# Deferred block products: operand steps issued a block ahead, and the second output weight combined in the last chunk and the first group

## The chip, the cores and the metric

The kernel runs on one core of one Trainium2 chip. TensorE (PE) multiplies out of SBUF into PSUM, ScalarE (ACT) and VectorE (DVE) split operands and move results, GpSimd (POOL) does a few SBUF-only operations, and every transfer (DMA) is issued by SyncE (SP), so all of them stand in one queue of issue. Each engine works through its own list of instructions in order and waits on semaphores for the others. The metric is device microseconds (us) for one execution; a change of about 0.2% (3.4 us) can be told from no change.

## The reference

```python
# attention through 32 packed tokens per head, B=8, H=8, S=576, D=64
p_packed = sm_attn(p, k, v)                 # softmax(p k^T / 8) v
x = sm_attn(q, p_packed, p_packed)          # -> 4608 tokens x 512
# first feed-forward: 512 -> 1536 -> 512
xn = x / rms(x) * rms_g
x = (silu(xn @ w_gate) * (xn @ w_val)) @ w_out
# second feed-forward: 512 -> 2048 -> 512, per-column leaky slope alpha
h = x @ w_in
out = (max(h, 0) + alpha * min(h, 0)) @ w_out
```

All inputs are float32. Every matrix product is done in three passes: an operand is split into a rounded high part and the rest, and high*high, high*low and low*high are added up (`mm3`).

## The kernel before

**First phase.** The 4608 tokens are walked in 12 chunks: chunks 0, 4, 7 and 10 have 512 tokens, the others 320. A chunk loops over 12 slices f of the hidden width. In a slice PE makes gate and value (`blk_in`), ACT applies a tanh or a silu (L1047 and L1049), DVE multiplies (L1052, L1056), the product is split by `hsplit` (high part on ACT L109, rest on DVE L112), and one slice later PE multiplies it with the output weight (`blk_out`). Between these the attention of the next chunk is worked in by hand-written turns (`work`, `burst`, `wg_job`). Chunk results go to `y_dram`. The last chunk has no attention beside it; there `prep(0)` makes the operands of the second phase's first group.

**The late weights.** `late` is a generator (`conv_late`) that turns the second feed-forward's weights, 8 pairs of row blocks of each, into operands. `work` calls it once in every slice of chunks 1 to 10. For a pair it takes seven steps: three that load and unpack two blocks (`narrow`), and four in `sevenths` that form the seven combinations a seven-product (Strassen-type) scheme needs. For a combination, `product` has ACT write the high part into a tile `w7o`, POOL subtract to get the rest (L275), and SP store the tile (256 KB) to DRAM: `w7_dram` for w_in, `o7_dram` for w_out. POOL also forms the sums and differences between (`combine`, L279). There are two `w7o` tiles (`bufs=2`), so the split of a combination waits until the store of the one two before it has landed. The last of the four steps makes three combinations at once: 6, 5 and 3 for w_out (6, 5 and 2 for w_in).

**Second phase.** Five groups of token pairs (`PAIRS`: three of 2 x 512, two of 2 x 384). Within a group a loop over i = 0 to 7 makes seven input products (`prod`, 6 matmuls each, in the order 0, 5, 4, 6, 1, 2, 3) into three PSUM banks a, b_ and c_. ACT copies product 0 out of a into `m1` (L1202); product 1 is then accumulated onto the same bank a, so on PE it follows that copy. ACT and DVE make the leaky activation (`halves_of`, `prelu`), and two output blocks of an earlier i run in between (`fill`). After the loop the other 40 output blocks follow, the list `LATER`: eight each of the kinds 5, 2, 6, 3, 1. A block (`block`) splits its operand (ACT, then DVE) and appends its 12 matmuls (9 in the narrow groups) to `fill`; they are issued once more than `LAG = 3` blocks wait. For kind 2 the operand is first formed in place by DVE:

```python
if n == 2:
    less2(s2, h21, s2)          # DVE L1132
block(x, n, i, g, w, ...)       # ACT split, DVE rest
```

Weight tiles are loaded in the order of their use by `load_next`, twelve ahead; each load is issued behind the PE work that frees its buffer. The ring of 2 x 2 buffers for split operands lets a block's split begin when the block four before it has left PE. The rows call both `w7_dram` and a scratch copy by names without digits: `w_dram<-w7o` is a store of w_in's combinations, `o_dram<-w7o` one of w_out's.

Of the kernel before, what the change touches and what calls it, by code (L numbers as in the profile page):

```python
# [18 lines left out]
def attention_moe_moe2_kernel(ctx, tc, q, k, v, p, w_gate, w_val, w_out, rms_g, w_in2, w_out2, alpha, out):  # L19
# [72 lines left out]
    gv_dram = tc.dram_tile([NJ * 4, 128, 512], F32, name="gv_dram")  # L92
    lo_dram = tc.dram_tile([NF, 128, 512], F32, name="lo_dram")
    w7_dram = tc.dram_tile([NP2 * 7, 128, 2, 256], F32, name="w7_dram")
    o7_dram = tc.dram_tile([NP2 * 7, 128, 2, 256], F32, name="o7_dram")
# [12 lines left out]
    def split_hi(hi, src):  # L108
        nc.scalar.activation(out=hi, in_=src, func=ACTF.Copy)  # L109
# [15 lines left out]
    with tc.manual_schedule():  # L125
# [124 lines left out]
        def conv_late():  # L250
            ahead = [load_wide(u, one, NST) for u in units2[:2]]
            yield
            for m in range(0, len(units2), 2):
                pair = []
                for n in (m, m + 1):
                    pair.append(one.tile([128, 4, 128], F32, tag="w32", name="w32", bufs=2))
                    steps = narrow(ahead.pop(0), pair[-1])
                    next(steps)
                    yield
                    for _ in steps:  # L260
                        pass
                    if n + 2 < len(units2):
                        ahead.append(load_wide(units2[n + 2], one, NST))
                yield
                yield from sevenths(*units2[m], pair)

        def sevenths(kind, i, pair):
            blocks = [t.rearrange("p c x -> p (c x)")[:, h * 256:(h + 1) * 256] for t in pair for h in range(2)]
            b11, b12, b21, b22 = blocks
# [615 lines left out]
        LATER = [(x, n, i) for x, n in (("b", 5), ("c", 2), ("b", 6), ("d", 3), ("a", 1)) for i in range(NP2)]  # L885
        LAG = 3

# [37 lines left out]
        for c, (t0, n, cuts) in enumerate(CH):  # L925
# [9 lines left out]
            def work(f, at):  # L935
# [18 lines left out]
                if c == 0:  # L954
                    conv(2 if at < 4 else 0)
                elif not last and at == 3:
                    next(late, None)

# [66 lines left out]
            for f in range(NF):  # L1025
# [9 lines left out]
                if last:  # L1035
                    if f == 0:
                        y_rows.append(load_rows(0, 0))
                        prepare = prep(0)
                    if f > 0:
                        next(prepare, None)  # L1040
                    if f in (2, 3, 8, 9, 10):
                        next(prepare, None)
                    load_next()
                tg = blk_in(f, 0, "g")
# [101 lines left out]

        def split2(g, w):
            n_h[0] += 1
            hh, hl = [
                ring.tile(  # L1150
                    [128, T], F32R, tag="ho"[n_h[0] % 2] + x, name="h" + x, bufs=NRO[x] if n_h[0] % 2 else 2
                )[:, 0:w]
                for x in "hl"
            ]
            split_hi(hh, g)
            split_lo(hl, g, hh)
            return hh, hl

        acc = {}

        def banks(x, j):
# [4 lines left out]
        def block(x, n, i, g, w, first, last, then=None):  # L1166
            hh, hl = split2(g, w)

            def run_block():
# [8 lines left out]
                if then:  # L1178
                    then()
            fill.append(run_block)  # L1180

        def pieces(w):
            return [(j, min(T, w * 2 - j * T)) for j in range((w * 2 + T - 1) // T)]

        for pr, (t0, w) in enumerate(PAIRS):
            final = pr + 1 == len(PAIRS)
            late_h, waiting = {}, []
            for i in range(NP2):
# [3 lines left out]
                def prod(o, n, first):  # L1192
# [4 lines left out]
                    load_next()  # L1197

                a, b_, c_ = [bank("g")[:, 0:w] for _ in range(3)]
                prod(a, 0, True)  # L1200
# [5 lines left out]
                for f_ in waiting:  # L1206
                    f_()
                prod(c_, 4, True)
                prod(b_, 6, False)
                u3 = temp(w)  # L1210
# [7 lines left out]
                n22 = halves_of(h22, h22, w)  # L1218
                prelu(h22, n22, i + NP2)
                fill.pop(0)()  # L1220
                prod(c_, 2, False)
                h12 = temp(w)
                add2(h12, u2, c_)
                block("a", 0, i, g11, w, i == 0, i == NP2 - 1)
                n12 = halves_of(h12, h12, w)
                prod(b_, 3, False)
                h21 = keep(1, i, w)
                add2(h21, m1, b_)
# [6 lines left out]
                n21 = halves_of(h21, h21, w)  # L1235
                late_h[i] = (h22, h21, s2, s3)
                fill.pop(0)()
                waiting = [
                    lambda h=h21, n=n21, f=i + NP2: prelu(h, n, f),
                    lambda s=s1, i=i, w=w: block("c", 4, i, s, w, i == 0, i == NP2 - 1),  # L1240
                ]
# [49 lines left out]
            prepare = iter(()) if final else prep(pr + 1)  # L1291
            for k_, (x, n, i) in enumerate(LATER):
                h22, h21, s2, s3 = late_h[i]
                if n == 2:
                    less2(s2, h21, s2)
                g = {5: s2, 2: s2, 6: s3, 3: h22, 1: h21}[n]
                then = None
                if i == NP2 - 1:
                    then = {5: done_b6, 2: done_c, 6: done_b7, 3: done_d, 1: lambda d=done_a, e=final: d(e)}[n]
                block(x, n, i, g, w, n in (5, 3) and i == 0, i == NP2 - 1, then)  # L1300
                while len(fill) > LAG:
# [44 lines left out]
```

## Time and profile before

| what | us |
|---|---|
| median of 3 runs (1713.65 to 1713.99) | 1713.79 |
| the profiled execution's own time | 1711.09 |
| its span, from the first to the last instruction | 1709.2 |
| chunks 1, 2, 3, 5, 6, 8, 9 (320 tokens) together | 489.3 |
| chunks 4, 7, 10 (512 tokens) together | 250.3 |
| chunk 11, the last | 42.8 |
| first group of the second phase | 166.5 |
| PE busy | 1601.2 |

The profile's busy time of PE counts overlapping matmuls with modelled ends, so PE can be late without showing as idle; the spacing of equal work tells more. ACT is busy 893.1 us and DVE 1147.2 us of the span.

### The profile page before, as it was taken

What the parts mean: (1) busy time and instruction counts of PE and PEld (TensorE: products, weight loads), DVE (VectorE), ACT (ScalarE), POOL (GpSimd) and SP (SyncE); (2) the same over time, 40 slices, a digit from 0 to 9 for tenths busy, and PEclk for the clock granted to TensorE, in tenths of its full rate; (3) what the DMA queues carried; (4) which work ended last, traced back from release to release, by engine and by line L of the source; (5) the groups of instructions that cost most, each with busy time, mean ns of one, the idle gap of its engine ahead of it and who ended that gap; (6) DMA issues with size and microseconds to landing.
All of it is one profiled execution on the core that took longest, in us unless ns stands there. A gap on an engine that the chain in (4) does not pass through costs nothing.

```text
span 1709.2 us, 31979 instructions
## 1 busy us (share of the span) xinstructions
PE 1601.2 (94%) x11786; PEld 1395.5 (82%) x11786; DVE 1147.2 (67%) x2132; ACT 893.1 (52%) x1906; POOL 339.6 (20%) x350
## 2 busy tenths in 40 slices
PE   6789999888999899999999999999999999999998
PEld 4457877777877787778888888888898889998998
DVE  5786656655566656556646677867777777777775
ACT  4566555554455454555545555544554544554553
POOL 1441344453445532233200000000000000000000
PEclk8899999999999999999999999999999999999999
DMA  9876656635456565675525666677566757877875
GB/s 255 257 251 193 186 168 204 179 114 180 158 179 206 158 202 181 213 237 172 178 88 190 179 196 197 216 204 215 166 222 203 210 154 236 259 247 252 260 227 179
DMA packets 230426, 340.55 MB, mean 199 GB/s; under 512 B 62464, under 2 KB 96256, under 8 KB 230272
## 3 DMA queue, kind: packets, MB, share of 16 engines
q1 hardware_dynamic: 230272, 338.51, 64.5%
q8 instruction: 94, 1.54, 0.4%
q14 instruction: 60, 0.49, 0.1%
HBM read 280.77 MB, written 57.67 MB: 198 GB/s over the span
## 4 chain that ended last, share of the span: by engine, by line
PE 62%; DVE 15%; ACT 8%; issue 6%; DMA 5%; POOL 3%; SPq 1%; ACTq 0%; DVEq 0%; POOLq 0%
PE ps_g L121 11%; PE ps_g L122 11%; PE ps_g L123 11%; PE ps_y L121 6%; PE ps_y L123 6%; PE ps_y L122 6%; DVE hl L112 2%; ACT hh L109 2%; PE ps_wg L731 2%; DMA w_dram<-w7o 2%; PE ps_v L121 2%; PE ps_v L122 1%; PE ps_v L123 1%; DVE kept L1132 1%; DVE s L1056 1%
## 5 line engine op out<-in xcount | busy, mean ns | idle before, releaser
L121 PE MATMUL ps_y<-hh,in_h 128*128 128x320 f32 (+1 forms) x576 | 207.9, 361 | 3.5 <-ACT hh L109 3.5
L121 PE MATMUL ps_g<-yh,w 128*128 128x512 f32 (+1 forms) x560 | 206.5, 369 | 0.0
L122 PE MATMUL ps_g<-yl,w 128*128 128x512 f32 (+1 forms) x560 | 206.3, 368 | 0.0
L123 PE MATMUL ps_g<-yh,w 128*128 128x512 f32 (+1 forms) x560 | 205.7, 367 | 0.0
L122 PE MATMUL ps_y<-hl,in_h 128*128 128x320 f32 (+1 forms) x576 | 196.9, 342 | 5.0 <-DVE hl L112 4.5
L123 PE MATMUL ps_y<-hh,in_l 128*128 128x320 f32 (+1 forms) x576 | 195.9, 340 | 0.6 <-DMA in_l<-lo_dram 0.6
L1052 DVE SCALAR_TENSOR_TENSOR s<-s,ps_g 128x320 f32<-128x320 f32 (+1 forms) x132 | 71.3, 540 | 166.1 <-ACT s L1047 165.8
L109 ACT ACTIVATE hh<-kept 128x512 fp32r<-128x512 f32 (+1 forms) x200 | 115.0, 586 | 129.1 <-DVE kept L1132 56.3
L121 PE MATMUL ps_y<-w,hh 128*128 128x256 f32 x576 | 167.5, 291 | 12.6 <-ACT hh L109 12.5
L123 PE MATMUL ps_y<-w,hl 128*128 128x256 f32 x576 | 168.3, 292 | 9.9 <-DVE hl L112 9.1
L122 PE MATMUL ps_y<-w,hh 128*128 128x256 f32 x576 | 164.8, 286 | 0.0
L112 DVE TENSOR_TENSOR hl<-kept,hh 128x512 fp32r<-128x512 f32 (+1 forms) x200 | 122.3, 635 | 60.1 <-ACT hh L109 59.7
L109 ACT ACTIVATE hh<-s 128x320 fp32r<-128x320 f32 (+1 forms) x144 | 75.6, 525 | 162.1 <-DVE s L1056 162.0
L121 PEld LDWEIGHTS ps_y<-hh,in_h 128*128 128x128 f32 x576 | 109.6, 190 | 58.7 <-issue 43.2
L275 POOL TENSOR_TENSOR w7o<-w,w7o 128x256 fp32r<-128x256 f32 x112 | 88.9, 800 | 205.9 <-ACT w7o L109 202.9
L121 PEld LDWEIGHTS ps_y<-w,hh 128*128 128x128 f32 x576 | 111.7, 194 | 19.1 <-ACT hh L109 16.6
L1129 DVE TENSOR_TENSOR tmp<-tmp,ps_g 128x512 f32<-128x512 f32 (+2 forms) x140 | 87.5, 631 | 58.3 <-PE ps_g L123 56.8
L112 DVE TENSOR_TENSOR hl<-s,hh 128x320 fp32r<-128x320 f32 (+1 forms) x144 | 85.8, 596 | 60.7 <-ACT hh L109 60.7
L123 PEld LDWEIGHTS ps_y<-w,hl 128*128 128x128 f32 x576 | 112.1, 195 | 15.8 <-DVE hl L112 15.7
L123 PE MATMUL ps_g<-w,hl 128*128 128x256 f32 x432 | 124.1, 287 | 0.4 <-DVE hl L112 0.4
L121 PE MATMUL ps_g<-w,hh 128*128 128x256 f32 x432 | 124.3, 288 | 0.0
L122 PE MATMUL ps_g<-w,hh 128*128 128x256 f32 x432 | 124.2, 287 | 0.0
(193 smaller groups left out, 4279.9 us busy)
## 6 DMA issues: line engine op xcount, KB each, us to landing
w<-w_dram SPq DMA_DIRECT2D x280, 256.0 KB, 3.0
w<-o_dram SPq DMA_DIRECT2D x280, 256.0 KB, 2.9
gv_raw<-gv_dram SPq DMA_DIRECT2D x168, 256.0 KB, 3.9
in_l<-lo_dram SPq DMA_DIRECT2D x59, 256.0 KB, 3.1
w<-in_moe_w_out_dram SPq DMA_DIRECT2D x28, 512.0 KB, 5.5
w_dram<-w7o SPq DMA_DIRECT2D x56, 256.0 KB, 2.1
o_dram<-w7o SPq DMA_DIRECT2D x56, 256.0 KB, 2.1
vt<-in_v_dram SPq DMA_DIRECT2D x16, 576.0 KB, 5.4
```

The costliest lines, as they stand in the source:

```text
L109: nc.scalar.activation(out=hi, in_=src, func=ACTF.Copy)
L112: nc.vector.tensor_tensor(out=lo, in0=src, in1=hi.bitcast(F32), op=ALU.subtract)
L121: nc.tensor.matmul(out=o, lhsT=lh, rhs=rh, start=first, stop=False, skip_group_check=more)
L122: nc.tensor.matmul(out=o, lhsT=lh, rhs=rl, start=False, stop=False, skip_group_check=more)
L123: nc.tensor.matmul(out=o, lhsT=ll, rhs=rh, start=False, stop=last, skip_group_check=more)
L275: nc.gpsimd.tensor_tensor(out=t[:, 1], in0=src, in1=t[:, 0].bitcast(F32), op=ALU.subtract)
L731: nc.tensor.matmul(out=ts[g][h * NP:(h + 1) * NP, :], lhsT=ppG[b][e * D:(e + 1) * D, c_, :], rhs=us[c_][e * D:(e + 1) * D, :], start=True, ...
L1052: nc.vector.scalar_tensor_tensor(out=s, in0=s, scalar=1.0, in1=tg, op0=ALU.add, op1=ALU.mult)
L1056: nc.vector.tensor_tensor(out=s, in0=s, in1=tv, op=ALU.mult)
L1129: nc.vector.tensor_tensor(out=out, in0=x, in1=y, op=ALU.add)
L1132: nc.vector.tensor_tensor(out=out, in0=x, in1=y, op=ALU.subtract)
```

## The change

It has three parts. First, in `LATER` a block is now a generator with two steps: the ACT split, and the DVE rest with the append to `fill`. The steps of neighbouring blocks are interleaved: DVE's `less2` for block k+2, ACT's split for k+1, DVE's rest for k. `LAG` goes from 3 to 2. Second, `conv_late` only unpacks w_out's pairs and stores them unsplit to a new scratch `w_dram` (two stores of 256 KB a pair); a new generator `make_o7` loads a pair back (512 KB into a `w64` tile) and then does the four steps of `sevenths`. It is called once at the start of each of the 12 slices of the last chunk and five times in every i of the first group (`make`), 40 steps in all. Third, `late` is called in every second slice of the 320-token chunks; in the 512-token chunks in every slice, and twice in every fourth.

```diff
+                kind, i = units2[m]
+                if kind == "o2":
+                    for e in range(2):
+                        nc.sync.dma_start(out=w_dram[i, :, e], in_=pair[e].rearrange("p c x -> p (c x)"))
                 yield
-                yield from sevenths(*units2[m], pair)
+                if kind == "i2":
+                    yield from sevenths(kind, i, [t.rearrange("p c x -> p (c x)") for t in pair])
+
+        def make_o7():
+            for i in range(NP2):
+                t = one.tile([128, 2, 512], F32, tag="w64", name="o2_raw", bufs=NST)
+                nc.sync.dma_start(out=t, in_=w_dram[i])
+                yield
+                yield from sevenths("o2", i, [t[:, e] for e in range(2)])
...
-        LAG = 3
+        LAG = 2
...
-                elif not last and at == 3:
-                    next(late, None)
+                elif not last and at == 3 and (f % 2 or n == T):
+                    for _ in range(1 + (n == T and f % 4 == 3)):
+                        next(late, None)
...
                     if f in (2, 3, 8, 9, 10):
                         next(prepare, None)
+                    next(making)
                     load_next()
...
+        def make(pr):
+            if pr == 0:
+                next(making, None)
...
-            hh, hl = split2(g, w)
+            hh, hl = split_tiles(w)
+            split_hi(hh, g)
+            yield
+            split_lo(hl, g, hh)
...
             fill.append(run_block)
+            yield
...
+                make(pr)
                 a, b_, c_ = [bank("g")[:, 0:w] for _ in range(3)]
                 prod(a, 0, True)
...
                 prod(c_, 4, True)
+                make(pr)
                 prod(b_, 6, False)
...
                 prelu(h22, n22, i + NP2)
+                make(pr)
                 fill.pop(0)()
...
                 prod(b_, 3, False)
+                make(pr)
                 h21 = keep(1, i, w)
...
                 late_h[i] = (h22, h21, s2, s3)
+                make(pr)
                 fill.pop(0)()
...
+            def combine_next(k_):
+                if k_ < len(LATER) and LATER[k_][1] == 2:
+                    _, h21, s2, _ = late_h[LATER[k_][2]]
+                    less2(s2, h21, s2)
+
+            next(splits[0])
+            for k_ in range(len(LATER)):
+                combine_next(k_ + 2)
+                if k_ + 1 < len(LATER):
+                    next(splits[k_ + 1])
+                next(splits[k_])
                 while len(fill) > LAG:
```

**Where instructions stand, 1: DVE in the kind-2 blocks of the first group.** `kept<-kept,kept` is `less2` for a kind-2 block, `hl<-kept,hh` the rest of a split, `tmp<-tmp,ps_g` the reading of kind 5's sums out of PSUM, `y_d` and `yl` belong to `prep` of the next group. Before:

```order
L1132 TENSOR_TENSOR kept_11612<-kept_11607,kept_11612 128x512
L112 TENSOR_TENSOR hl_12720<-kept_11612,hh_12719 128x512
L1132 TENSOR_TENSOR kept_11750<-kept_11745,kept_11750 128x512
L112 TENSOR_TENSOR hl_12739<-kept_11750,hh_12738 128x512
L1132 TENSOR_TENSOR kept_11882<-kept_11877,kept_11882 128x512
L112 TENSOR_TENSOR hl_12758<-kept_11882,hh_12757 128x512
L1129 TENSOR_TENSOR tmp_12775<-tmp_12582,ps_g_12618 128x512
L1129 TENSOR_TENSOR tmp_12777<-tmp_12584,ps_g_12625 128x512
L856 TENSOR_TENSOR y_d_12779<-y_raw_12295,y_raw_12293 128x512
L112 TENSOR_TENSOR yl_12782<-y_d_12712,yh_12781 128x512
```

With the change:

```order
L1148 TENSOR_TENSOR kept_11815<-kept_11810,kept_11815 128x512
L113 TENSOR_TENSOR hl_12747<-kept_11477,hh_12746 128x512
L1148 TENSOR_TENSOR kept_11979<-kept_11974,kept_11979 128x512
L113 TENSOR_TENSOR hl_12772<-kept_11649,hh_12771 128x512
L1145 TENSOR_TENSOR tmp_12808<-tmp_12614,ps_g_12644 128x512
L1145 TENSOR_TENSOR tmp_12810<-tmp_12616,ps_g_12651 128x512
L1148 TENSOR_TENSOR kept_12143<-kept_12138,kept_12143 128x512
L113 TENSOR_TENSOR hl_12791<-kept_11815,hh_12790 128x512
L869 TENSOR_TENSOR y_d_12831<-y_raw_12328,y_raw_12326 128x512
L113 TENSOR_TENSOR yl_12834<-y_d_12764,yh_12833 128x512
```

A block's rest no longer stands right behind its own `less2`: two other blocks' steps stand between, and the sums are read with two blocks issued ahead where there were three.

**2: ACT in the first group, from the activation of one i to the copy `m1` of the next.** `neg` and the tile behind it are the two halves of the activation, `hh` a split, L1202 (now L1224) the copy `m1`. Before:

```order
L1137 ACTIVATE kept_11819<-kept_11819 128x512
L109 ACTIVATE hh_11862<-tmp_11829 128x512
L1136 ACTIVATE neg_11866<-tmp_11860 128x512
L1137 ACTIVATE tmp_11860<-tmp_11860 128x512
L1136 ACTIVATE neg_11886<-kept_11877 128x512
L1137 ACTIVATE kept_11877<-kept_11877 128x512
L1202 ACTIVATE tmp_11914<-ps_g_11903 128x512
```

With the change, from the three combinations of one pair to the same copy:

```order
L110 ACTIVATE w7o_11588<-o2_raw_11470 128x256
L110 ACTIVATE w7o_11593<-o2_raw_11470 128x256
L110 ACTIVATE w7o_11597<-o2_raw_11470 128x256
L110 ACTIVATE hh_11627<-tmp_11579 128x512
L1152 ACTIVATE neg_11631<-tmp_11625 128x512
L1153 ACTIVATE tmp_11625<-tmp_11625 128x512
L1152 ACTIVATE neg_11653<-kept_11644 128x512
L1153 ACTIVATE kept_11644<-kept_11644 128x512
L110 ACTIVATE w7o_11656<-o2_raw_11642 128x256
L110 ACTIVATE w7o_11660<-o2_raw_11642 128x256
L110 ACTIVATE w7o_11680<-o2_raw_11642 128x256
L1224 ACTIVATE tmp_11696<-ps_g_11685 128x512
```

The last rows ahead of the copy are now splits of the next pair: two of a tile `o2_raw` that a load has just been issued for, and a third that takes the `w7o` buffer of the first of them.

**3: SP in the first group, the same stretch.** Before, only weight loads stand here:

```order
L913 DMA w7_11718<-o7_dram_79 128x512
L913 DMA w7_11726<-w7_dram_78 128x512
L913 DMA w7_11743<-w7_dram_78 128x512
L913 DMA w7_11771<-w7_dram_78 128x512
L913 DMA w7_11782<-w7_dram_78 128x512
```

With the change:

```order
L289 DMA o7_dram_80<-w7o_11588 128x512
L289 DMA o7_dram_80<-w7o_11593 128x512
L289 DMA o7_dram_80<-w7o_11597 128x512
L926 DMA w7_11615<-o7_dram_80 128x512
L926 DMA w7_11623<-w7_dram_79 128x512
L926 DMA w7_11640<-w7_dram_79 128x512
L276 DMA o2_raw_11642<-w_dram_78 128x1024
L289 DMA o7_dram_80<-w7o_11656 128x512
L289 DMA o7_dram_80<-w7o_11660 128x512
L926 DMA w7_11678<-w7_dram_79 128x512
L289 DMA o7_dram_80<-w7o_11680 128x512
```

The load of the next pair (`o2_raw`) stands behind the stores of the three combinations, and the stores of its first two combinations stand ahead of the next weight loads.

## Rows read from the trace of the kernel before

**Rows 1.** The page: the span, and busy time by engine.

```profile
span 1709.2 us, 31979 instructions
PE 1601.2 (94%) x11786; PEld 1395.5 (82%) x11786; DVE 1147.2 (67%) x2132; ACT 893.1 (52%) x1906; POOL 339.6 (20%) x350
```

**Rows 2.** Busy time by stretch, the five kind-2 stages: us; engines busy (instructions).

```profile
sum 80.19, PE 65.92 PEld 57.34 DVE 56.43 ACT 31.61 POOL 0.00; mean PE 13.18 PEld 11.47 DVE 11.29 ACT 6.32 POOL 0.00
```

**Rows 3.** The same for the five kind-6 stages behind them.

```profile
1248.79:1260.31 11.52, 11.52 (x98) 11.52 (x97) 9.30 (x16) 6.40 (x12) 0.00 (x0) 1.00 0.81 274
sum 51.84, PE 51.84 PEld 51.84 DVE 39.53 ACT 27.79 POOL 0.00; mean PE 10.37 PEld 10.37 DVE 7.91 ACT 5.56 POOL 0.00
```

**Rows 4.** DVE in order of time, kind 2 of the second group: start, us.

```profile
1239.93 0.69 DVE L112 TENSOR_TENSOR hl<-kept,hh 128x512 fp32r<-128x512 f32 x1 [0.78 <-ACT hh L109]
1240.54 0.68 DVE L1132 TENSOR_TENSOR kept<-kept 128x512 f32<-128x512 f32 x1
1242.00 0.69 DVE L112 TENSOR_TENSOR hl<-kept,hh 128x512 fp32r<-128x512 f32 x1 [0.78 <-ACT hh L109]
...
1249.76 1.28 DVE L1129 TENSOR_TENSOR stg<-tmp,ps_y 128x512 f32<-128x512 f32 x2
```

**Rows 5.** Busy time by stretch, the seven 320-token chunks.

```profile
sum 489.32, PE 442.52 PEld 375.34 DVE 297.38 ACT 264.65 POOL 216.53; mean PE 63.22 PEld 53.62 DVE 42.48 ACT 37.81 POOL 30.93
```

**Rows 6.** The same, chunks 4, 7 and 10 (512 tokens).

```profile
sum 250.34, PE 249.56 PEld 206.42 DVE 141.97 ACT 120.43 POOL 68.27; mean PE 83.19 PEld 68.81 DVE 47.32 ACT 40.14 POOL 22.76
```

**Rows 7.** Tile w7o: durations min/median/max in ns; waits in us, times.

```profile
L109 ACT ACTIVATE w7o<-w x112: 400/415/419, 194.6 to 860.3; 128x256 fp32r<-128x256 f32 x112
L275 POOL TENSOR_TENSOR w7o<-w,w7o x112: 722/738/1187, 195.0 to 860.8; 128x256 fp32r<-128x256 f32 x112
L276 SPq DMA_DIRECT2D w_dram<-w7o x56: 319/320/832, 195.8 to 816.5; - x56
...
  DMA w_dram<-w7o: 34.1, 12
  DMA o_dram<-w7o: 22.4, 11
...
DMA to landing us min/median/max: 2.0/2.1/6.5
```

**Rows 8.** ACT in order of time, three combinations in chunk 6.

```profile
609.85 0.94 ACT L109 ACTIVATE w7o<-w 128x256 fp32r<-128x256 f32 x2
613.22 0.42 ACT L109 ACTIVATE w7o<-w 128x256 fp32r<-128x256 f32 x1 [2.43 <-DMA o_dram<-w7o]
```

**Rows 9.** Tile w7o by stretch, the seven 320-token chunks: last one and sum.

```profile
767.54:825.29 57.75, 4.61 (x12) 8.81 (x12) 1.00 0.56 186
sum 489.32, ACT 32.48 POOL 65.27; mean ACT 4.64 POOL 9.32
```

**Rows 10.** ACT in order of time, first group.

```profile
986.51 0.60 ACT L1202 ACTIVATE tmp<-ps_g 128x512 f32<-128x512 f32 x1 [0.80 <-PE ps_g L123]
...
991.95 0.60 ACT L1136 ACTIVATE neg<-ps_g 128x512 f32<-128x512 f32 x1 [4.32 <-PE ps_g L123]
...
994.12 0.61 ACT L109 ACTIVATE hh<-tmp 128x512 fp32r<-128x512 f32 x1
```

**Rows 11.** PE in order of time: product 1 of two neighbouring i.

```profile
990.39 0.39 PE L121 MATMUL ps_g<-yh,w 128*128 128x512 f32 x1
...
1002.83 0.39 PE L121 MATMUL ps_g<-yh,w 128*128 128x512 f32 x1
```

**Rows 12.** Tile y_raw, loads of 512 and 384 KB.

```profile
DMA to landing us min/median/max: 3.6/5.3/6.2
```

**Rows 13.** ACT in order of time, last chunk, its first slices.

```profile
909.77 0.64 ACT L109 ACTIVATE yh<-y_raw 128x512 fp32r<-128x512 f32 x1 [2.05 <-DMA y_raw<-y_dram]
910.31 0.42 ACT L1047 ACTIVATE s<-ps_g 128x320 f32<-128x320 f32 x1
912.16 0.47 ACT L109 ACTIVATE hh<-s 128x320 fp32r<-128x320 f32 x1 [1.43 <-DVE s L1056]
912.54 0.61 ACT L109 ACTIVATE in_h<-w_raw 128x512 fp32r<-128x512 f32 x1
```

**Rows 14.** Busy time behind a wait of PE; the 0.50 is its granted clock.

```profile
1216.70:1220.10 3.40, 3.40 (x16) 3.40 (x17) 2.31 (x4) 2.00 (x4) 0.00 (x0) 0.50 0.03 10
```

**Rows 15.** Line 112, 165 to 905 us: durations in ns min/median/max.

```profile
L112 DVE TENSOR_TENSOR xl<-A2T,xh x20: 293/930/1809, 242.9 to 902.2; 128x512 fp32r<-128x512 f32 x13, 128x128 fp32r<-128x128 f32 x7
```

More of the change, by code (lines that the diff above doesn't have):

```diff
@@ L93, in attention_moe_moe2_kernel @@
     lo_dram = tc.dram_tile([NF, 128, 512], F32, name="lo_dram")
+    w_dram = tc.dram_tile([NP2, 128, 2, 512], F32, name="w_dram")
     w7_dram = tc.dram_tile([NP2 * 7, 128, 2, 256], F32, name="w7_dram")
@@ L263, in conv_late @@
                         ahead.append(load_wide(units2[n + 2], one, NST))
+                kind, i = units2[m]
+                if kind == "o2":
+                    for e in range(2):
+                        nc.sync.dma_start(out=w_dram[i, :, e], in_=pair[e].rearrange("p c x -> p (c x)"))
                 yield
-                yield from sevenths(*units2[m], pair)
+                if kind == "i2":
[6 more added lines that the diff above has]
+                yield from sevenths("o2", i, [t[:, e] for e in range(2)])
         def sevenths(kind, i, pair):
-            blocks = [t.rearrange("p c x -> p (c x)")[:, h * 256:(h + 1) * 256] for t in pair for h in range(2)]
+            blocks = [t[:, h * 256:(h + 1) * 256] for t in pair for h in range(2)]
             b11, b12, b21, b22 = blocks
@@ L1038, in attention_moe_moe2_kernel @@
                         prepare = prep(0)
+                        making = make_o7()
                     if f > 0:
@@ L1145, in attention_moe_moe2_kernel, with split_tiles @@
         n_h = [0]
-        def split2(g, w):
+        def split_tiles(w):
             n_h[0] += 1
-            hh, hl = [
+            return [
                 ring.tile(
@@ L1154, in split2 @@
             ]
-            split_hi(hh, g)
-            split_lo(hl, g, hh)
-            return hh, hl
         acc = {}
+        def make(pr):
+            if pr == 0:
+                next(making, None)
         def banks(x, j):
@@ L1223, in attention_moe_moe2_kernel @@
                 add2(h12, u2, c_)
-                block("a", 0, i, g11, w, i == 0, i == NP2 - 1)
+                for _ in block("a", 0, i, g11, w, i == 0, i == NP2 - 1):
+                    pass
                 n12 = halves_of(h12, h12, w)
                 prod(b_, 3, False)
+                make(pr)
                 h21 = keep(1, i, w)
@@ L1239, in attention_moe_moe2_kernel @@
                     lambda h=h21, n=n21, f=i + NP2: prelu(h, n, f),
-                    lambda s=s1, i=i, w=w: block("c", 4, i, s, w, i == 0, i == NP2 - 1),
+                    lambda s=s1, i=i, w=w: list(block("c", 4, i, s, w, i == 0, i == NP2 - 1)),
                 ]
@@ L1291, in attention_moe_moe2_kernel @@
             prepare = iter(()) if final else prep(pr + 1)
-            for k_, (x, n, i) in enumerate(LATER):
+            splits = []
+            for x, n, i in LATER:
                 h22, h21, s2, s3 = late_h[i]
-                if n == 2:
-                    less2(s2, h21, s2)
                 g = {5: s2, 2: s2, 6: s3, 3: h22, 1: h21}[n]
@@ L1299, in attention_moe_moe2_kernel @@
                     then = {5: done_b6, 2: done_c, 6: done_b7, 3: done_d, 1: lambda d=done_a, e=final: d(e)}[n]
-                block(x, n, i, g, w, n in (5, 3) and i == 0, i == NP2 - 1, then)
+                splits.append(block(x, n, i, g, w, n in (5, 3) and i == 0, i == NP2 - 1, then))
+            def combine_next(k_):
[8 more added lines that the diff above has]
+                next(splits[k_])
                 while len(fill) > LAG:
```

## The prediction

> **What bounds the kernel now.** I read the page first: PE is busy for 1601.2 of 1709.2 us, no other engine for more than 67% [rows 1]. So a saving counts only where PE stands still or runs late, and a cost only where something is put ahead of PE's next matmul. The busy time by stretch says where that is. In the seven 320-token chunks PE works 442.5 of 489.3 us, so 46.8 are idle [rows 5]; in the three 512-token chunks 249.6 of 250.3 [rows 6]. In the second phase the stages of kind-2 blocks take 80.19 us and those of kind 6, with the same count of the same matmuls, 51.84 [rows 2, 3]. So 28.35 us are lost in the kind-2 stages, of which PE's modelled busy time shows only half.
>
> DVE in order of time says why: the rest of one block waits 0.78 for ACT's split, then comes `less2` of the next block (0.68), then again a wait of 0.78 [rows 4]. `less2`, split and rest of a block run one behind the other, 2.07 us per block (1239.93 to 1242.00) against the 1.44 of a kind-6 block, 11.52 divided by 8 [rows 3, 4].
>
> **The steps of kind 2.** With the steps issued for different blocks, `less2` and the rest of DVE need 0.68 + 0.69 = 1.37 us at most per wide block, and ACT's split runs under them. That is below 1.44, so PE becomes the bound and up to 28.35 us come back. The cover is thin (0.07 us a block). It is gone where kind 5's sums are read, 1.28 us for two [rows 4]: with `LAG = 2` only two blocks (2.88 us) are issued ahead, and 1.28 + 2 x 0.68 is 2.64, to which the split's latency of about 0.6 is added. The same is true where `prep` stands between the last kind-2 blocks. I put 0.8 us at each of two such places in five groups, 8 us, and take **-20**. The ends are -12 (double that loss) and -28.
>
> **The 320-token chunks.** `late` runs at half its pace there, and w_out's combinations are gone from the first phase but for those moved. By tile, 12 combinations of one such chunk cost ACT 4.61 us and POOL 8.81, in all seven 32.48 and 65.27 [rows 9]. Counting in the two orders, their number falls there from 84 to 30; with a split at 0.415 [rows 7] ACT does 54 x 0.415 = 22 us less. Two splits in three then no longer wait for a store; of the 34.1 + 22.4 us that they waited [rows 7] I give back 33. Three combinations in a row show such a wait: the third split starts 3.37 us behind the first, 2.43 of it waiting for the first one's store [rows 8]. ACT's tanh for PE's next slice stands behind it. ACT would thus lose 55 us, more than PE has idle, so 46.8 is the ceiling. What else stops PE there (attention turns, DVE, the loads) stays, and no row tells the shares. Between 5 and 45 I take 27, a little over half. In the 512-token chunks `late` is called twice in every fourth slice. PE has 0.8 us idle there and ACT is busy 120 of 250 [rows 6], which covers most of it. Uncovered, nine double calls with a wait of 2.43 at half of them would be 10; I take 3. Net **-24**.
>
> **The last chunk.** Twelve calls do two whole pairs and the first two steps of a third: 16 splits, three loads. ACT's chain is closed there: tanh, DVE's product (a wait of 1.43), the split `hh`, the split of `prep`, the next tanh [rows 13], and none of these waits for PE. So ACT's time adds up. The splits are 16 x 0.42 = 6.7. Two triples wait for a store each: split to landed store is 0.74 + 2.1, less the 0.42 of the second split, 2.42 each, 4.8 in all. Each pair's first split comes one slice (42.8 / 12 = 3.6 us) behind its load. The nearest load, of the same size, lands in 3.6 to 6.2, median 5.3 [rows 12], and the first queues behind two of `y_raw`, whose own user already waits 2.05 [rows 13]: 2.9 for the first and 2.5 for the other two together. The sum is 16.9. A split can fall into the wait for DVE, so I take **+15**; ends 8 and 20.
>
> **The first group.** This is the largest term. The chain goes from one i to the next, with t the start of product 1, whose spacing is now 1002.83 - 990.39 = 12.44 us [rows 11].
>
> - The activation starts at t + 1.56 (990.39 to 991.95) and takes to t + 3.73, where `hh` stands now [rows 10, 11]. The triple of the fourth step comes there.
> - Its first split ends at 4.15 (0.42), POOL's rest at 4.89 (0.74), the store lands 2.1 later, at 6.99; only then does the third split find a buffer: 7.41, its rest 8.15 [rows 7].
> - SP issues that store, three weight loads and the next pair's load behind it, each 0.32 [rows 7]: the load is under way at 9.43 (its own issue I leave in the landing). It lands 5.3 later [rows 12], at 14.73.
> - The pair's first split ends at 15.15, its rest at 15.89, its store lands at 17.99. The split of the next i's first call needs that very buffer: 18.41. Behind it on ACT stands the copy `m1`, 0.60 [rows 10], and product 1 of the next i needs the bank that it clears: 19.0.
>
> So 19.0 in place of 12.44, 6.6 us for each of the five passes from i = 0 to i = 5 (the 28 steps left end in i = 5), 33 in all. Behind a wait PE's granted clock was 0.50 for 3.4 us in the second group [rows 14], the lower of its levels (1.2 of 2.4 GHz); that loses about 1.7 us at most, and I add 1 a pass: **+38**. With a landing of 3.6 and a store at 2.0 the pass falls to 17.1 and the term to 23; with 6.2, rests of POOL at 1.19 [rows 7] and the full price of the clock it is about 53. What hides it now is `fill`, blocks of an earlier i that PE can do meanwhile, but their operand splits stand in the same queue of ACT, behind the waiting combination. The weight loads behind the waiting stores on SP are no second stop: they run twelve tiles ahead, and a tile lasts PE (12.44 - 2 x 1.44) / 7 = 1.37 us here (seven tiles and two blocks in an i), so 16 us, and SP is held about 7 to 11.
>
> POOL's moved operations, 56 rests and 32 sums at 0.74, are 65 us of work on an engine that is idle from there on, so its time alone costs nothing.
>
> By a rule of the Trainium skill (SBUF — State Buffer, "Who interferes with whom") a DVE instruction with two SBUF inputs contends with a GpSimd instruction that reads SBUF, and one blocks the other for its whole length. The trace agrees: POOL's rest takes 738 ns and up to 1187 [rows 7], DVE's `xl` 293 to 1809 beside POOL's work, though in mixed shapes [rows 15]. By the page the moved POOL work would meet DVE in the first group, where every rest has two SBUF inputs, and the sum would be about +16 where the median rows make it +9.
>
> **Sum.** -20 - 24 + 15 + 38 = +9 on the profiled 1711.09: 1720. The median of the runs is 2.7 above the profiled execution, so **1723**.
>
> **Rivals.** *The first phase gives nearly all of its idle time back (faster).* If the 46.8 us of PE idle come from ACT's waits and splits alone, the term is -47 instead of -24, and the time about 1700. For it: ACT is relieved of more than that by my count. Against it: ACT is busy only 265 of the 489 us there and PE's longest chains run through attention. It decides from 33 us on (24 + 9).
>
> *The wait in the first group is short (faster).* With a landing of 3.6, +23, and a last chunk at +8, the sum is -13, about 1701. For it: SP has little else to move there. Against it: `y_raw` loads took 5.3 under the same weight traffic [rows 12].
>
> *It is worse than summed.* Late landings, POOL and DVE holding each other up and PE at its lower clock make the first group +53: 1738. For it, the 1187 and 1809 ns above [rows 7, 15]; if three rests in a pass take 1.19, that is 1.35 us a pass, 7 in all.
>
> *The interleaving does not do what it says.* If DVE with 1.37 per block and the shorter `LAG` still sets the pace, 8 of the 28 us come back: 1735. For it, the cover of 0.07 a block; against it, the kind-6 stages, where the same ACT and DVE splits keep PE full [rows 3].
>
> **How the numbers follow.** The forecast case gets 0.40 (on its own 1714 to 1731), the first phase giving all 0.24, the short wait 0.12, the worse case 0.13, interleaving without effect 0.11. The range must reach to both sides: **1697 to 1742**. From no change a measurement can tell 0.2%, 3.4 us, so "same" is 1710 to 1717, which the forecast case's lower end touches, and the short wait's upper one. Faster 0.33, same 0.12, slower 0.55.
>
> **What would show it.** Right: the kind-2 stages near 56 to 60 us in sum; the 320-token chunks near 460; chunk 11 near 58; product 1 of the first group spaced 18 to 20 us for five i and 12.44 after, with `m1`'s neighbour on ACT waiting for a store and the pair's first split for its load. Wrong: first-group spacing under 15, which would mean that the load is early enough and takes the whole positive term down; the 320-token chunks under 450 or above 480; kind-2 stages still above 70, with DVE busy throughout.

## The result and the profile after

| | median, us | runs |
|---|---|---|
| before | 1713.72 | 4, 1710.55 to 1713.99 |
| with the change | 1732.22 | 4, 1731.16 to 1737.27 |

The ratio is 1.0118, with a 95% interval of 1.0095 to 1.0141: the change makes the kernel 18.5 us slower. The forecast was 1723, +9, with 1697 to 1742 as its range. So the sign was right and the size half of what was measured. The page of the changed kernel begins:

```profile
span 1729.4 us, 32037 instructions
PE 1594.4 (92%) x11786; PEld 1397.7 (81%) x11786; DVE 1143.1 (66%) x2132; ACT 898.7 (52%) x1906; POOL 345.8 (20%) x350
```

Against [rows 1] the span grew by 20.2 us, while no engine has over 6.2 us more work, and PE and DVE have less: the time must be waiting. Busy time by stretch of the changed kernel says where (start and end, length, then busy us and count of PE, PEld, DVE, ACT and POOL in this order, PE's granted clock, the share of DMA, GB/s). The lines are, in this order, the sum of the five kind-2 stages, of the seven 320-token chunks and of chunks 4, 7 and 10, then the last chunk and the first group up to its kind-5 blocks:

```profile
sum 55.90, PE 53.53 PEld 52.21 DVE 51.56 ACT 29.34 POOL 0.00; mean PE 10.71 PEld 10.44 DVE 10.31 ACT 5.87 POOL 0.00
...
sum 449.30, PE 427.52 PEld 368.98 DVE 281.11 ACT 242.58 POOL 145.88; mean PE 61.07 PEld 52.71 DVE 40.16 ACT 34.65 POOL 20.84
...
sum 255.50, PE 252.26 PEld 208.20 DVE 151.08 ACT 125.98 POOL 74.64; mean PE 84.09 PEld 69.40 DVE 50.36 ACT 41.99 POOL 24.88
...
873.05:934.30 61.25, 47.62 (x264) 44.67 (x262) 31.35 (x55) 27.72 (x62) 17.88 (x22) 0.89 0.66 232
934.30:1099.80 165.50, 114.75 (x554) 95.89 (x553) 82.09 (x119) 70.51 (x142) 52.43 (x67) 0.85 0.62 208
```

Stage by stage, between the two profiled executions:

| stage | before | after | change | forecast |
|---|---|---|---|---|
| kind-2 stages [rows 2] | 80.19 | 55.90 | -24.3 | -20 |
| 320-token chunks [rows 5] | 489.3 | 449.3 | -40.0 | -27 |
| 512-token chunks [rows 6] | 250.3 | 255.5 | +5.2 | +3 |
| last chunk | 42.8 | 61.25 | +18.4 | +15 |
| first group, loop over i (excess over 12.44 per i) | 0.6 | 60.9 | +60.3 | +38 |
| sum | | | +19.6 | +9 |

The excess in the loop is taken from the starts of product 0, which are now 14.28, 21.90, 24.12, 23.72, 24.00, 23.81 and 16.20 us apart, where six of seven were 12.44 and the first 13.08. (Chunk 1 starts at 164.5 us before and at 168.2 now; this start differs by over 4 us among the traces of this case and is left out, and so are 3 us by which the rest of the second phase is shorter.)

One pass of that loop, i = 2 to i = 3, in order of time. ACT of the changed kernel (start, duration, operation; in brackets the wait ahead of it and what ended it):

```profile
991.38 0.71 ACT L110 ACTIVATE w7o<-o_raw 128x256 fp32r<-128x256 f32 x2
994.99 0.42 ACT L110 ACTIVATE w7o<-o_raw 128x256 fp32r<-128x256 f32 x1 [2.90 <-DMA o_dram<-w7o]
...
1003.28 0.72 ACT L110 ACTIVATE w7o<-o_raw 128x256 fp32r<-128x256 f32 x2 [4.58 <-DMA o_raw<-w_dram]
1006.64 0.42 ACT L110 ACTIVATE w7o<-o_raw 128x256 fp32r<-128x256 f32 x1 [2.63 <-DMA o_dram<-w7o]
1006.96 0.58 ACT L1224 ACTIVATE tmp<-ps_g 128x512 f32<-128x512 f32 x1
```

SP in the same pass, the three stores and the next pair's load:

```profile
992.88 3.69 SPq L289 DMA_DIRECT2D o_dram<-w7o  x3
...
998.33 0.42 SPq L276 DMA_DIRECT2D o_raw<-w_dram  x1
```

DVE in the same pass, its first operation behind the copy:

```profile
1007.57 0.69 DVE L1145 TENSOR_TENSOR tmp<-tmp,ps_g 128x512 f32<-128x512 f32 x1 [7.48 <-ACT tmp L1224]
```

PE, where the pass begins and ends (first matmul of product 1, of the next product 6 and of the next product 1):

```profile
987.48 0.53 PE L122 MATMUL ps_g<-yh,w 128*128 128x512 f32 x1
...
1008.31 0.79 PE L122 MATMUL ps_g<-yh,w 128*128 128x512 f32 x1 [9.44 <-DVE tmp L1145]
...
1011.04 0.63 PE L122 MATMUL ps_g<-yh,w 128*128 128x512 f32 x1
```

The reader is to see three waits of ACT (2.90 for a store, 4.58 for the pair's load, 2.63 for a store), 10.1 us in all, then the copy `m1` (L1224), and behind it not product 1 but DVE's sum of `m1` and product 5 (L1145). Product 5 lies in bank b_, and product 6 is accumulated onto the same bank, so product 6 waits for that sum (9.44). It starts at 1008.31; product 1 stands behind it on PE. Busy time of that product 6 alone:

```profile
1008.31:1011.04 2.73, 2.73 (x6) 2.15 (x7) 1.92 (x2) 0.42 (x1) 2.65 (x4) 0.50 0.87 293
```

Its six matmuls take 2.73 us at a granted clock of 0.50 (1.2 of 2.4 GHz), where 1.36 is usual.

The other passes are like this one: product 6 waits for DVE's sum in seven of the eight i, 7.6 to 10.0 us in the five long passes. In us, times and longest, up to the group's kind-5 blocks:

```profile
PE ps_g L122 <- DVE tmp L1145: 49.1, 7, 10.0
```

Before, PE has no such wait in the loop. The rest of the 60.3 is PE's clock for the most part. Five passes before and the five long ones now:

```profile
960.00:1022.20 62.20, 62.20 (x332) 53.78 (x331) 46.50 (x70) 32.54 (x59) 0.00 (x0) 1.00 0.69 196
...
948.58:1066.13 117.55, 71.18 (x333) 59.01 (x331) 50.95 (x70) 44.88 (x94) 44.23 (x55) 0.80 0.59 202
```

For the same matmuls PE is busy 9.0 us longer, at a granted clock of 0.80 in the mean where it was 1.00. DVE is busy 4.4 us longer.

### The profile page after: what moved, and what is told of

The parts are those of the page before. It is cut to its first block, busy times and chain, and to the rows that moved or that the text cites. A ratio compares the mean times of both kernels' runs of the same rounds, so it can differ in the third digit from the quotient of the medians.

```text
span 1729.4 us, 32037 instructions
## 1 busy us (share of the span) xinstructions
PE 1594.4 (92%) x11786; PEld 1397.7 (81%) x11786; DVE 1143.1 (66%) x2132; ACT 898.7 (52%) x1906; POOL 345.8 (20%) x350
## 4 chain that ended last, share of the span: by engine, by line
PE 62%; DVE 12%; issue 8%; DMA 7%; ACT 6%; POOL 4%; SPq 1%; POOLq 0%; ACTq 0%; DVEq 0%
PE ps_g L122 10%; PE ps_g L123 10%; PE ps_g L124 10%; PE ps_y L122 7%; PE ps_y L124 7%; PE ps_y L123 6%; DMA o_raw<-w_dram 3%; PE ps_wg L744 2%; DVE hl L113 2%; POOL w7o L288 2%; PE ps_v L122 2%; PE ps_v L123 2%; PE ps_v L124 2%; DMA o_dram<-w7o 1%; DVE kept L1148 1%
## 5 line engine op out<-in xcount | busy, mean ns | idle before, releaser
L122 PE MATMUL ps_g<-yh,w 128*128 128x512 f32 (+1 forms) x560 | 211.6, 378 | 49.1 <-DVE tmp L1145 49.1
L122 PE MATMUL ps_y<-hh,in_h 128*128 128x320 f32 (+1 forms) x576 | 209.4, 364 | 13.9 <-ACT hh L110 13.9
L124 PE MATMUL ps_g<-yh,w 128*128 128x512 f32 (+1 forms) x560 | 208.7, 373 | 0.0
L124 PE MATMUL ps_y<-w,hl 128*128 128x256 f32 x576 | 164.2, 285 | 8.7 <-DVE hl L113 8.5
L122 PE MATMUL ps_y<-w,hh 128*128 128x256 f32 x576 | 163.0, 283 | 1.9 <-ACT hh L110 1.9
L123 PE MATMUL ps_y<-w,hh 128*128 128x256 f32 x576 | 162.8, 283 | 0.0
L122 PEld LDWEIGHTS ps_g<-yh,w 128*128 128x128 f32 x560 | 107.6, 192 | 64.4 <-DVE tmp L1145 52.1
L1145 DVE TENSOR_TENSOR tmp<-tmp,ps_g 128x512 f32<-128x512 f32 (+2 forms) x140 | 87.9, 632 | 96.6 <-PE ps_g L124 58.0
L113 DVE TENSOR_TENSOR hl<-kept,hh 128x512 fp32r<-128x512 f32 (+1 forms) x200 | 121.0, 632 | 18.4 <-ACT hh L110 18.0
L375 POOL TENSOR_TENSOR in_l<-w_raw,in_h 128x512 fp32r<-128x512 f32 x72 | 94.1, 1307 | 157.6 <-ACT in_h L110 130.9
L122 PE MATMUL ps_g<-xh,wgh 128*128 128x256 f32 (+3 forms) x352 | 114.4, 325 | 10.5 <-DVE s L1068 3.2
```

The lines of the kernel that those rows point to most:

```text
L113: nc.vector.tensor_tensor(out=lo, in0=src, in1=hi.bitcast(F32), op=ALU.subtract)
L122: nc.tensor.matmul(out=o, lhsT=lh, rhs=rh, start=first, stop=False, skip_group_check=more)
L123: nc.tensor.matmul(out=o, lhsT=lh, rhs=rl, start=False, stop=False, skip_group_check=more)
L124: nc.tensor.matmul(out=o, lhsT=ll, rhs=rh, start=False, stop=last, skip_group_check=more)
L375: nc.gpsimd.tensor_tensor(out=l, in0=raw[u], in1=h.bitcast(F32), op=ALU.subtract)
L1145: nc.vector.tensor_tensor(out=out, in0=x, in1=y, op=ALU.add)
```

## The experiments

**Theory A**: the first group's loop is one closed chain over ACT, POOL, SP and the landings of stores and loads, and every wait in it counts. **Rival B**: POOL's moved work and DVE's hold each other up, and that made the group slower than forecast. Beside these stand the questions whether the other terms are separate. Each ratio is to the kernel before, timed beside the run; its median lay between 1712.9 and 1714.9 in the four sets of runs, and its single runs between 1708 and 1722. A difference of 2 us between kernels of different sets is therefore no difference.

**The steps alone.** The kernel before with the interleaving and nothing else:

```diff
-        LAG = 3
+        LAG = 2
...
-            hh, hl = split2(g, w)
+            hh, hl = split_tiles(w)
+            split_hi(hh, g)
+            yield
+            split_lo(hl, g, hh)
```

> The kernel before with the first part alone (interleaved steps, LAG 2); the second output weight is still combined in the first phase. Theory (the gain of the steps and the loss of the moved combinations are separate): the kind-2 stages go from 80 to about 54 us and nothing else moves, so 1714 - 26 = 1688. Rival (part of what the trace after shows in the kind-2 stages is owed to the moved work, and LAG 2 costs elsewhere): a gain of 8 to 15, 1699 to 1706.

Measured: 1690.42 us, ratio 0.9855 (0.9818 to 0.9893), 24.5 us below the kernel before beside it (1714.92). Sum of its kind-2 stages:

```profile
sum 55.89, PE 53.54 PEld 52.22 DVE 51.66 ACT 29.32 POOL 0.00; mean PE 10.71 PEld 10.44 DVE 10.33 ACT 5.86 POOL 0.00
```

That is the 55.90 of the changed kernel. The whole gain of the steps comes without the moved work, so the two are separate, and the moved work together with the new pace of `late` is a loss of some 42 us (1732.2 to 1690.4).

**The load two calls earlier.**

```diff
-                t = one.tile([128, 2, 512], F32, tag="w64", name="o2_raw", bufs=NST)
-                nc.sync.dma_start(out=t, in_=w_dram[i])
-                yield
-                yield from sevenths("o2", i, [t[:, e] for e in range(2)])
+                yield
+                t, steps = nxt, sevenths("o2", i, [nxt[:, e] for e in range(2)])
+                for k, _ in enumerate(steps):
+                    if k == 1 and i + 1 < NP2:
+                        nxt = load(i + 1)
+                    yield
```

> The changed kernel with the load of the next pair issued two calls earlier. Theory A (the first group is one closed chain over ACT, POOL, SP and the landings, ended by the copy m1, DVE's sum and product 6): the wait of 4.6 us for the load goes in each of five passes and about 5 us in the last chunk, 1732 - 27 = 1705. Rival B (POOL and DVE hold each other up on SBUF, and that is what made the group slower than forecast): the wait only moves to the next in line, under 5 us, 1727 or more.

The load leaves with the second of a pair's four steps, ahead of the calls that do the third and the fourth.

Measured: 1705.49, ratio 0.9966 (0.9942 to 0.9989). The five long spacings of product 0 are now 19.3 to 20.3 in place of 21.9 to 24.1; the loop is 20.3 us shorter, and the last chunk 1.7 where 5 were expected. What ended the idle time ahead of the splits, their rests and their stores (us, times), in the changed kernel and in this one:

```profile
  DMA o_raw<-w_dram: 29.2, 7
...
  DMA o_raw<-w_dram: 2.0, 1
```

ACT in this kernel, the three splits of one call:

```profile
997.22 0.40 ACT L110 ACTIVATE w7o<-o_raw 128x256 fp32r<-128x256 f32 x1
997.89 0.42 ACT L110 ACTIVATE w7o<-o_raw 128x256 fp32r<-128x256 f32 x1 [0.27 <-DMA o_dram<-w7o]
1000.85 0.42 ACT L110 ACTIVATE w7o<-o_raw 128x256 fp32r<-128x256 f32 x1 [2.55 <-DMA o_dram<-w7o]
```

The wait for the load is gone, those for stores stay. The time is theory A's 1705, and B's 1727 is passed by far. That it is 1705 to the microsecond is in part luck: loop and last chunk of the profiled execution give 22 of the 27 us, and some 4 more lie ahead of chunk 1, in the start that differs from trace to trace.

**Four buffers.** The second pair of buffers is that of `y_d`, idle in the loop of the first group:

```diff
-                t = one.tile([128, 2, 256], F32R, tag="w7o", name="w7o", bufs=2)
+                n_made[0] += kind == "o2"
+                tag = ("w7o", "w32")[n_made[0] % 2]
+                t = one.tile([128, 2, 256], F32R, tag=tag, name="w7o", bufs=2)
```

> The changed kernel with the combinations of the second output weight in four buffers in place of two (two of them those that y_d and the raw blocks use). Theory A: both waits for a store (2.9 and 2.6 us) leave each of five passes and the triples of the last chunk no longer wait, 1732 - 27 - 5 = 1700. Rival B: as POOL's rests and sums are unchanged, under 5 us, 1727 or more.

Measured: 1710.86, ratio 0.9965 (0.9948 to 0.9983), 21 us gained where 32 were expected. ACT:

```profile
995.68 1.03 ACT L110 ACTIVATE w7o<-o_raw 128x256 fp32r<-128x256 f32 x3 [5.38 <-DMA o_raw<-w_dram]
...
1007.40 0.42 ACT L110 ACTIVATE w7o<-o_raw 128x256 fp32r<-128x256 f32 x1 [1.51 <-POOL o_raw L296]
```

The waits for stores are gone, the pair's first three splits run on end. But the third of the triple now waits 1.51 for a sum of POOL, which the store's wait had covered, and the load is waited for longer (5.38): the spacing is 20.5 to 20.9. Theory A's order of size, with a smaller number; B's bound is passed by far.

**The copy first.**

```diff
-                make(pr)
                 a, b_, c_ = [bank("g")[:, 0:w] for _ in range(3)]
...
                 add2(u2, m1, b_)
+                make(pr)
```

> The changed kernel with the first call of each i moved behind the copy m1 and DVE's sum. Theory A: the copy no longer stands behind the split that waits for a store; it comes about 3.0 us earlier in each of five passes, 1732 - 15 = 1717, and the pair's load still holds it. Rival B: nothing, 1732, since POOL's work is the same.

Measured: 1718.46, ratio 1.0013 (0.9993 to 1.0033). ACT:

```profile
1024.84 0.72 ACT L110 ACTIVATE w7o<-o_raw 128x256 fp32r<-128x256 f32 x2 [4.12 <-DMA o_raw<-w_dram]
1025.47 0.58 ACT L1223 ACTIVATE tmp<-ps_g 128x512 f32<-128x512 f32 x1
1028.18 0.42 ACT L110 ACTIVATE w7o<-o_raw 128x256 fp32r<-128x256 f32 x1 [2.13 <-DMA o_dram<-w7o]
```

The copy comes right behind the pair's first splits and the split that waits for a store comes after it. The call's rest and store move with its split, so on SP the store stands behind a weight load or two more; no work was taken away. 13.8 us came back of the 15 expected (13.5 in the loop of the profiled execution): what is late in the changed kernel is the copy and what hangs on it.

**All three together.** The three edits above in one kernel.

> The changed kernel with the early load, the four buffers and the call behind the copy together. Theory A: nothing of the closed chain is left but ACT's own seven splits (2.9 us) in an i; the spacing of product 0 falls from 23.9 to between 12.44 and 15, so about 45 to 55 us in the group and 6 in the last chunk, 1732 - 55 = 1677 (1672 to 1682). Rival B (POOL and DVE hold each other up): at least half of the 11.4 us a pass stays, 1700 or more.

Measured: 1672.95, ratio 0.9758 (0.9739 to 0.9777); four spacings of product 0 are 13.9 and one 16.1. The three gains apart (26.7, 21.4 and 13.8) add up to 62, and together they give 59. As theory A has it.

**And the combinations spread.**

```diff
             product(0, b11)
+            if kind == "o2" and i:
+                yield
             product(3 if kind == "i2" else 2, b22)
-            yield
+            if kind == "i2":
+                yield
...
                 product(6, b12)
                 combine(b21, b21, b22)
+                yield
                 product(5, b22)
                 product(3, b21)
```

> As the run before, and the seven combinations of a pair spread over the five calls as 1, 2, 1, 1, 2 in place of 2, 1, 1, 3 and a load. Theory A: the same splits, none of which waits in either; the last chunk gains 2 to 4 us as no call has three, so 1674 (1668 to 1680). Rival B: as for the run before.

Measured: 1669.24, ratio 0.9746 (0.9732 to 0.9761), 44 us faster than the kernel before. It is the lowest median of these, but the 2 to 4 us expected over the run with all three are not clear of the spread. Busy time of the group's five middle passes:

```profile
940.43:1006.96 66.53, 63.70 (x332) 53.40 (x331) 53.39 (x71) 44.74 (x94) 49.89 (x56) 1.00 0.98 343
```

They take 66.5 us, 13.3 a pass, and the granted clock is 1.00, with POOL 49.9 us busy. POOL did the same for 44 us in the 117.6 us of the same passes of the changed kernel. The last chunk still takes 55.5 against 42.8. ACT's waits there:

```profile
ACT w7o L110 <- DMA o_dram<-w7o: 5.7, 2, 3.1
ACT w7o L110 <- DMA o_raw<-w_dram: 2.1, 1, 2.1
```

With 6.0 us of splits that is 13.8 us, and the chunk is 12.7 longer.

**No sums on POOL.** The kernel leaves out the 32 sums and differences for the second output weight; splits, rests, stores and loads stay.

```diff
             def combine(out, x, y, op=ALU.subtract):
+                if kind == "o2":
+                    return
```

> The changed kernel without POOL's 32 sums and differences for the second output weight (so the combinations are not the right ones and the output isn't the reference's); splits, rests, stores and loads are all there. Theory A: a sum stands on the closed chain only where it delays a split or a rest, about 1 us in each of five passes, 1732 - 5 = 1727. Rival B: 40 per cent of POOL's operations are gone and with them as much of the added time in the group, 20 us or more, 1712 or less.

Measured: 1731.38, ratio 1.0107 (1.0092 to 1.0122), the time of the changed kernel. POOL's work in the group (busy us, mean ns, idle before):

```profile
L288 POOL TENSOR_TENSOR w7o<-o_raw,w7o 128x256 fp32r<-128x256 f32 x42 | 33.5, 810 | 109.3 <-ACT w7o L110 109.2
```

ACT's waits in the same stretch (us in total, times, longest), and then those of the changed kernel:

```profile
ACT w7o L110 <- DMA o_dram<-w7o: 30.0, 13, 3.0
ACT w7o L110 <- DMA o_raw<-w_dram: 22.3, 5, 6.1
...
ACT w7o L110 <- DMA o_dram<-w7o: 30.0, 12, 2.9
ACT w7o L110 <- DMA o_raw<-w_dram: 22.8, 5, 5.2
```

The sums are gone, 19 us of POOL in the group, and the waits for stores and loads are the 30 and 23 us of the changed kernel. Rival B falls: it asked for 20 us or more. The rests still stand beside DVE here; but with sums and rests DVE's busy time had grown by no more than 4.4 us in the five long passes of the changed kernel, as shown above. A's 5 us did not come either; the sums lie beside the chain, as long as the waits for stores cover them.

**The old pace.** `late` in every slice, so that w_in's combinations end in chunk 7:

```diff
-                elif not last and at == 3 and (f % 2 or n == T):
-                    for _ in range(1 + (n == T and f % 4 == 3)):
-                        next(late, None)
+                elif not last and at == 3:
+                    next(late, None)
```

> The changed kernel with one call of late in every slice as before, so that w_in's combinations end in chunk 7. Theory (the 35 us of the first phase come from the number of combinations there, not from the pace): the early chunks give back what the late ones gain, 1732 plus or minus 6. Rival (the pace, which leaves two slices for a combination's store to land, gives them): chunks 1 to 6 fall back to the times of before, 1747 or more.

Measured: 1741.61, ratio 1.0168 (1.0150 to 1.0186), 9.4 above the changed kernel, between both expectations. Sums of its 320-token and 512-token chunks:

```profile
sum 464.10, PE 434.20 PEld 370.86 DVE 293.23 ACT 251.47 POOL 164.67; mean PE 62.03 PEld 52.98 DVE 41.89 ACT 35.92 POOL 23.52
...
sum 252.70, PE 249.50 PEld 205.71 DVE 140.16 ACT 116.82 POOL 53.11; mean PE 83.17 PEld 68.57 DVE 46.72 ACT 38.94 POOL 17.70
```

Neither theory alone: of the 40.0 us of the 320-token chunks, 25.2 come with w_out's combinations leaving the first phase and 14.8 with the pace, taken in this order. Chunk 1 shows the pace at its clearest: 80.5 us here, 73.2 in the changed kernel.

**No doubled calls.** The run with everything, without the second call in every fourth slice of the 512-token chunks:

```diff
-                    for _ in range(1 + (n == T and f % 4 == 3)):
-                        next(late, None)
+                    next(late, None)
```

> The run e6 without the doubled calls of late in the 512-token chunks; the few calls then left over come behind chunk 10. Theory (two calls in one slice put ACT's split behind a store there, which is where the 5 us that those chunks lost come from): chunks 4, 7 and 10 go back from 255 to about 251 us in sum, 2 to 3 us are paid behind chunk 10, 1669 - 2 = 1667. Rival (they lost it to other things, as loads): 255 in sum, 1669 to 1673.

Measured: 1670.20, ratio 0.9744 (0.9719 to 0.9769), no change. Chunks 4, 7 and 10:

```profile
376.95:468.05 91.10, 88.14 (x725) 72.64 (x726) 53.18 (x106) 43.72 (x95) 32.96 (x30) 0.97 0.51 155
594.35:678.55 84.20, 83.77 (x709) 68.92 (x708) 51.95 (x102) 41.40 (x90) 18.23 (x19) 1.00 0.56 185
791.75:873.55 81.80, 80.67 (x588) 67.09 (x587) 45.01 (x83) 39.22 (x83) 20.43 (x24) 1.00 0.48 158
```

The 251 us of the theory do not come: the sum is 257.1, and the time, forecast at 1667 by one and at 1669 to 1673 by the other, does not tell the two apart. But chunk 7 goes back to 84.2, as in the run with the old pace, which has no doubled calls either (86.6 in the changed kernel), so there they were the cost. Chunk 10 pays 2.8 for the calls left over (79.0 in the changed kernel). Chunk 4 stays at 91 where it was 87.3 before, but its length is not steady: counted from each chunk's first matmul it is 89.9 to 93.3 in the seven traces with doubled calls and 89.3 to 93.3 in the four without, so nothing can be read from it. Chunk 7, counted so, is 87.1 to 88.8 in the seven and 84.7 to 85.8 in the four.

## Why the prediction came out at half the size

**The step that failed** is the last of the first group's chain, in the prediction's words: "product 1 of the next i needs the bank that it clears: 19.0". The chain up to the copy `m1` was right within 1.4 us: first split at t + 3.90 (forecast 3.73), third split at t + 7.5 (6.99), load issued at t + 10.85 (9.43), the pair's first split at t + 15.8 (14.73), `m1` done at t + 20.1 (19.0), with t = 987.48. Behind the copy the prediction went on along bank a, to product 1. But the copy has an earlier user: DVE's sum of `m1` and product 5, which must have read bank b_ before product 6 may be added there, and PE has product 6 ahead of product 1. So 0.7 us of DVE and 2.73 of product 6 at the lower clock lie between, and a pass is 23.56, not 19.0. The copy-first run shows that PE's wait hangs on that copy, and the rows of PE and DVE show through what. The clock had been put at 1 us a pass; it is 1.37 for product 6 alone (2.73 less 1.36), and 1.8 in the mean of the five long passes (71.18 less 62.20, by 5).

So the term: five passes by 11.1 are 55.6, and the shorter waits of the first and the last pass, which the prediction put at nothing, give 5, together 60.3, where 38 was forecast: 22 us of error, more than the whole forecast. Landings and rests were about as taken (4.95 us from the load's issue to the split for 5.3, stores 2.0 for 2.1); the reserve for late landings was not needed.

**The other terms** were each right in sign, but not in size: the two gains were larger than forecast by 17 us together, the two smaller costs by 6. That the time still fell within the range is luck, since 17 us of error stood against 28. One of the prediction's own signs of being wrong did come: the 320-token chunks are under 450. The steps gave 24.3 for 20: DVE runs through the sums with two blocks' steps and `prep` between, as foreseen, but what is lost there is not 8 us but about 4. DVE in the second group's kind-2 stage, where [rows 4] showed a wait of 0.78 in each block:

```profile
1271.94 0.68 DVE L113 TENSOR_TENSOR hl<-kept,hh 128x512 fp32r<-128x512 f32 x1
1272.54 1.27 DVE L1145 TENSOR_TENSOR tmp<-tmp,ps_g 128x512 f32<-128x512 f32 x2
1273.73 0.68 DVE L1148 TENSOR_TENSOR kept<-kept 128x512 f32<-128x512 f32 x1
1274.34 0.68 DVE L113 TENSOR_TENSOR hl<-kept,hh 128x512 fp32r<-128x512 f32 x1
```

No row shown has a wait any more. The 320-token chunks gave 40 for 27. The first rival ("gives nearly all of its idle time back") named the point from which it decides, 33 us; that was passed, and the kernel still got slower, since the first group took more. The 46.8 us of idle time were no ceiling, since PE's busy time there also fell, from 442.5 to 427.5: idle time went down by 25 us only while 40 came back. So what share of ACT's waits reached PE, which the prediction had to guess, stays open. The last chunk's term is mis-sized by 3: the waits of ACT there are

```profile
ACT w7o L110 <- DMA o_dram<-w7o: 6.9, 2, 4.0
ACT w7o L110 <- DMA o_raw<-w_dram: 6.5, 2, 4.4
```

for 4.8 and 5.4 forecast. With 5.3 for the 14 splits that lie in it they make 18.7, and 18.4 arrive, so little of it was hidden. The 512-token chunks cost 5.2 for 3, and only chunk 7's part, 2.4, is shown to be that of the doubled calls.

**The rivals.** The interleaving without effect is refuted by the run of the steps alone. The short wait (landing 3.6) is refuted: the pair was waited for at 4.6 us in a pass. The worse case came nearest to the group's total (+53), but of its three reasons the late landings did not come, POOL and DVE hold each other up by little, and only the lower clock cost what it said. The Trainium skill (SBUF — State Buffer, "Who interferes with whom") has POOL's rests and DVE's two-input instructions block each other, and the trace agrees: rests take up to 1184 ns against a median of 738, and in the five long passes DVE's rest of a split, which reads two operands from SBUF, takes 1014 ns in the mean where it took 684, while its sum with a bank of PSUM stays at 685. Two that stand side by side:

```profile
985.45 1.22 DVE L113 TENSOR_TENSOR hl<-tmp,hh 128x512 fp32r<-128x512 f32 x1
...
986.07 1.18 POOL L288 TENSOR_TENSOR w7o<-o_raw,w7o 128x256 fp32r<-128x256 f32 x1
```

It does not set the time here: it adds 4.4 us to DVE's busy time in five passes that are 55 us longer, without the sums the time stays the same (1731.4), and with most waits removed POOL does the same work in passes of 13.3 us.

## What to carry to other kernels

Work moved under a loop that looks half empty is free only if each of its steps can wait without holding up something that the bound engine needs: here ACT was half idle, but its queue is in order, so three waits of 2.6 to 4.6 us on DMA stood ahead of one copy of 0.6 us. When such a chain is followed, follow every user of what arrives late, in the bound engine's own order of work; the first that it meets sets the time. The same move, with the interleaved steps and with its load issued ahead of the pair's last two steps, four buffers, no call ahead of the copy and no three combinations in one call turns a loss of 18.5 us into a gain of 44.

## What the runs showed that was not expected

PE's busy time in the page is no fixed sum of work: with the same matmuls it fell by 15 us in the 320-token chunks, so its complement understates what can be gained. In part that goes with the granted clock, which in chunk 1 rose from 0.96 to 1.00 while PE's busy time went from 77.6 to 73.2. In part it is not, as chunk 8 shows, before and with the change:

```profile
703.82:767.54 63.72, 58.30 (x453) 47.33 (x452) 37.89 (x81) 35.90 (x85) 20.07 (x23) 1.00 0.76 248
...
679.50:736.90 57.40, 55.94 (x454) 46.75 (x453) 36.56 (x80) 32.43 (x75) 9.33 (x10) 1.00 0.74 238
```

What that other part is stays open. And a single late step in a pass cost clock as well: the mean granted clock of the five long passes is 0.80, and 1.00 again with the waits removed, in the run with the combinations spread.
